# Another buffer for the second chunk's q, new durations for the norm's steps in a plan, and a new table of places (four interleaved attention layers, one core)

## The chip, the cores and the metric

The kernel runs on one core of a Trainium2 chip. Its engines are PE (TensorE, matrix products), DVE (VectorE), ACT (ScalarE), POOL (GpSimd) and SP (SyncE, which here only issues DMAs). The metric is the device time of one execution in microseconds; a kernel's time is the median of several runs.

## What is computed

Four layers in the order A, B, A, B are added to x, which has 2048 rows of 512 values in f32. Each layer is x + attention(layernorm(x)), with 32 heads of 16:

```python
def _A_ref(x, wqkv, wo):          # H = 32, Dh = 16, W = 8, dil = 2
    q, k, v = split(x @ wqkv)
    idx = pos[:, None] - off[None, :]      # off = 0, 2, ..., 14
    logits = einsum("bhsd,bhswd->bhsw", q, k[idx]) * scale
    attn = softmax(where(idx >= 0, logits, -1e9))
    return merge(einsum("bhsw,bhswd->bhsd", attn, v[idx])) @ wo
...
def _B_ref(x, wqkv, wo):          # W = 256
    scores = einsum("bhqd,bhkd->bhqk", q, k) * scale
    mask = (0 <= i - j) & (i - j < 256)
    p = softmax(where(mask, scores, -1e9))
    return merge(einsum("bhqk,bhkd->bhqd", p, v)) @ wo
...
x = x + _A_ref(_layernorm(x), A_wqkv, A_wo)
x = x + _B_ref(_layernorm(x), B_wqkv, B_wo)
x = x + _A_ref(_layernorm(x), A_wqkv, A_wo)
x = x + _B_ref(_layernorm(x), B_wqkv, B_wo)
```

In A each row looks at itself and seven rows before it, two apart; in B at the 256 rows that end with itself.

## The kernel before

Each layer is worked in eight chunks of 256 rows. A chunk of an A layer and a chunk of the B layer behind it run interleaved, so that the chunks of one layer's products fill the time of the other's elementwise work; a layer's next chunk starts when the rows that it needs are there. Products with weights are made of fp16 parts, high and low, so one product is three matmuls (L1014, L1015, L1016 with rows along the free axis; L1036, L1037, L1034 for the output projection).

The norm of a chunk: ACT makes the mean (L935) and the sum of squares (L938) of each of its two tiles of 128 rows, POOL makes from them the variance (L941), its root's inverse (L944) and the shift (L947). ACT normalizes (xn, L963 or L985) and casts to the high part (ht, L973); the remainder xn − ht (L969) runs on POOL or on DVE. In a layer A both parts go through DMAs that transpose them (xh, xl); for the first chunk and layer B, PE transposes (L989) and ACT and DVE cast (xh L994, xl L995).

A chunk of layer A then: PE makes q, k and v transposed, ACT copies q (L1130) and k, v with their halo (kv, L1132; halo copies L1122 and L1139 on POOL). For each of four groups of 128 channels (m = 0 to 3) and each of four stretches of 64 rows a product of q with the eight keys of its window (pr, L1151, 16 per chunk, 128x512, on DVE or POOL) is made, and PE reduces it over the 16 values of a head with a matrix of ones (L1159, four matmuls a group). The softmax over 8 is on DVE: maximum L1182, difference L1185, sum L1188, reciprocal L1191, scaling L1194, with the exponential on ACT (L1211); the result is cast (eh, L1215) and its remainder e − eh taken (L1202, DVE or POOL). PE spreads the weights over the heads' values (L1228), DVE weighs v (pw, L1241, eight per chunk, 128x1024), and the sums are taken on DVE (L1246) or in three steps on POOL (L1248, L1249, L1250). The finish: high part oh (L1058, ACT), remainder ol (L1060, DVE or POOL), projection, and the sum with x (y, L1068, DVE).

A chunk of layer B: k and q as high and low parts (eh L1272, el L1275), through DRAM into stacks (DMAs re L1285, stk L1296, both from SP's queue); a first pass of scores for the rows' maxima (L1338, L1341 on PE; mask and maximum L1359 and L1355 on DVE, or L1351 alone for a chunk without full tiles), the maxima transposed and split (mr L1374, mt L1381 to L1384) and added to the product by another row of the stack, the scores (L1431, L1433), the exponential (p, L1437, ACT), the mask (L1446, POOL), the product with v (L1463), and the division (os, L1480 to L1489).

What sets the order: every step is added to a plan with an engine, a duration in us, and what it reads and writes. Its place on its engine comes from a table, `ORDER[scope]`, by the step's number in its scope (the scopes are S, pA and pB for masks and weights, W for 110 groups of three idle matmuls, L1578, and A0 to A15, B0 to B15 for the chunks of the two A and the two B layers). A negative number puts the step on its second engine at place −1 − p. Each engine runs its steps strictly in the order of places. The durations serve `Plan.order()` alone: it plays the engines' queues against each other, gives buffers and PSUM banks as they come free in that play, and so sets the order in which the program is written and which bank a step gets.

Buffers come from pools by tag, in rotation. `po4` has one buffer for each of its tags: q, oa and ob. q of each A chunk takes the tag q, so a chunk's q may be written when the products of the chunk before have read theirs. `pp6` has one tag, p6, with three buffers of the same size: the staging of the output weights in the weight preparation, and later the probabilities p of layer B.

## Time and profile before

| | us |
|---|---|
| three runs: median (lowest to highest) | 1425.57 (1422.78 to 1426.98) |
| the profiled execution's own time | 1422.53 |
| its span in the profile | 1420.8 |
| PE busy in it | 1331.4 |
| DVE busy | 1125.9 |
| ACT busy | 818.9 |
| POOL busy | 697.2 |

The profile is one execution. Its span runs from the first to the last instruction that the profile shows, 1.7 us less than the execution's time. The mean granted clock of PE was 0.962 of the full one. "Busy" counts an engine's working instructions, not its waits and not the issuing of DMAs. A row of a view by line gives line, engine, operation, output and inputs with their shapes, how often, then the busy time of all, the mean of one in ns, the idle time of the engine just before them, and what ended that idle time.

The steps of the norm, whose durations in the plan the change sets anew, took in the trace: L935 628 ns with a read of its sum of 188 to 192 behind it, L938 720 with 188, L941 274, L944 741, L947 277, all means of 32 or 64.

### The profile page before, as it was taken

Reading aid. Unit: us, or ns where it says so; the run is one execution under the profiler, and the core shown is the slowest. Engines: PE = TensorE matmul, PEld = TensorE weight load, DVE = VectorE, ACT = ScalarE, POOL = GpSimd, SP = SyncE. Lnnn points to the kernel's source line nnn. Section 1 sums busy time; section 2 is a strip of 40 time slices with the busy share of each in tenths; the row PEclk is TensorE's granted clock in tenths of the full one; section 3 lists DMA queues with packets and bytes.
Section 4 is the critical chain, followed back from the end, with each engine's and each line's share of the span. In section 5 each row is a group of like instructions: output and inputs, shape, how many; then the busy total and the mean of one; then the engine's idle time right before and its main releaser. Section 6 shows DMA issues by size and latency. Waiting matters only on the chain.

```text
span 1420.8 us, 35345 instructions
## 1 busy us (share of the span) xinstructions
PE 1331.4 (94%) x13918; PEld 782.5 (55%) x13918; DVE 1125.9 (79%) x2087; ACT 818.9 (58%) x1297; POOL 697.2 (49%) x836
## 2 busy tenths in 40 slices
PE   9986989999899999999999898999989999998997
PEld 7642647456374654637465373745637465473644
DVE  7978796977969788796967759597796968879693
ACT  8732555565576557565675445656467555646564
POOL 4425182653747345373664627464272744738232
PEclk9996999999999999999999899998999999999999
DMA  8232333142342333324142252323324233233221
GB/s 267 67 101 58 108 66 104 47 103 85 97 132 49 105 84 88 101 73 137 45 116 78 59 136 67 108 77 88 99 74 135 53 92 87 72 107 85 95 73 58
DMA packets 135944, 130.46 MB, mean 92 GB/s; under 512 B 68448, under 2 KB 94560, under 8 KB 135776
## 3 DMA queue, kind: packets, MB, share of 16 engines
q1 hardware_dynamic: 135520, 127.93, 33.2%
q8 instruction: 109, 1.79, 0.5%
q14 instruction: 59, 0.48, 0.1%
q10 hardware_dynamic: 256, 0.26, 0.1%
HBM read 67.11 MB, written 43.48 MB: 78 GB/s over the span
## 4 chain that ended last, share of the span: by engine, by line
PE 60%; DVE 14%; POOL 7%; DMA 5%; issue 5%; ACT 5%; SPq 3%; DVEq 0%; POOLq 0%; ACTq 0%
PE banks L1014 9%; PE banks L1015 8%; PE banks L1016 8%; PE banks L1463 7%; PE banks L1036 5%; PE banks L1034 4%; PE banks L1431 4%; PE banks L1037 4%; PE banks L1159 4%; DVE m L1355 3%; PE banks L1338 3%; DVE pw L1241 3%; POOL pw L1248 3%; ACT p L1437 3%; PE banks L1341 2%
## 5 line engine op out<-in xcount | busy, mean ns | idle before, releaser
L1437 ACT ACTIVATE p<-banks,sclB 128x768 f32<-128x768 f32 x480 | 419.4, 901 | 246.5 <-PE banks L1433 172.8
L1446 POOL TENSOR_SCALAR_AFFINE_SELECT p<-p 128x1024 f32<-128x1024 f32 x240 | 262.8, 1103 | 315.7 <-ACT p L1437 304.1
L1355 DVE TENSOR_REDUCE m<-banks 128x2 f32<-128x512 f32 x448 | 296.0, 686 | 3.6
L1359 DVE COPY_PREDICATED banks<-maskt,banks 128x256 f32<-128x256 int16 x448 | 177.6, 423 | 72.3 <-PE banks L1341 57.6
L1463 PE MATMUL banks<-p,v 128*32 128x128 f32 (+1 forms) x3840 | 196.9, 334 | 5.3 <-POOL p L1446 4.7
L1151 DVE TENSOR_TENSOR pr<-kv,q 128x512 f32<-128x512 f32 x222 | 155.7, 752 | 42.9 <-PE banks L1159 27.8
L1463 PEld LDWEIGHTS banks<-p,v 128*32 128x32 f32 x3840 | 107.0, 110 | 96.7 <-issue 35.7
L1431 PE MATMUL banks<-stk,stk 64*128 64x256 f16 x960 | 133.3, 285 | 27.1 <-ACT p L1437 10.7
L1241 DVE TENSOR_TENSOR pw<-banks,kv 128x1024 f32<-128x1024 f32 x128 | 153.1, 1215 | 4.2 <-POOL o L1250 2.4
L1341 PE MATMUL banks<-stk,stk 48*128 48x128 f16 (+1 forms) x1024 | 127.0, 251 | 16.2 <-DVE m L1351 10.3
L1248 POOL TENSOR_TENSOR pw<-pw 128x512 f32<-128x512 f32 x100 | 127.2, 1272 | 10.5 <-DVE pw L1241 10.3
L1338 PE MATMUL banks<-stk,stk 48*128 48x256 f16 (+1 forms) x896 | 110.2, 253 | 18.0 <-DVE m L1355 9.4
L1431 PEld LDWEIGHTS <-stk 64*128 64x128 f16 x960 | 56.6, 95 | 121.4 <-issue 114.6
L1433 PE MATMUL banks<-stk,stk 64*128 64x128 f16 x960 | 108.2, 224 | 0.0
L1275 DVE SCALAR_TENSOR_TENSOR el<-banks,eh 128x512 f16<-128x512 f32 x64 | 43.2, 688 | 79.3 <-ACT eh L1272 49.9
L1338 PEld LDWEIGHTS <-stk 48*128 48x128 f16 x896 | 50.4, 95 | 94.3 <-issue 88.3
L1249 POOL TENSOR_TENSOR pw<-pw 128x256 f32<-128x256 f32 x100 | 72.7, 727 | 7.8
L1341 PEld LDWEIGHTS <-stk 48*128 48x128 f16 x1024 | 52.9, 96 | 35.2 <-issue 32.0
L1015 PE MATMUL banks<-xl,wA1h 128*128 128x256 f16 x256 | 69.8, 273 | 1.9 <-DMA xl<-xn 1.9
L1159 PE MATMUL banks<-pr,sel 128*32 128x512 f32 x512 | 70.6, 603 | 0.9 <-DVE y L1068 0.9
L1014 PE MATMUL banks<-xh,wA0h 128*128 128x256 f16 x256 | 70.1, 274 | 0.6 <-DMA xh<-ht 0.3
L1014 PE MATMUL banks<-xh,wA2h 128*128 128x256 f16 x256 | 70.4, 275 | 0.0
(201 smaller groups left out, 3110.8 us busy)
## 6 DMA issues: line engine op xcount, KB each, us to landing
stk<-re SPq DMA_DIRECT2D x256, 96.0 KB
re<-eh SPq DMA_DIRECT2D x128, 128.0 KB
xm<-y SPq DMA_DIRECT2D x32, 256.0 KB
re<-el SPq DMA_DIRECT2D x64, 128.0 KB
y<-xm SPq DMA_DIRECT2D x32, 256.0 KB
oc<-os SPq DMA_DIRECT2D x120, 64.0 KB
os<-scr SPq DMA_DIRECT2D x15, 512.0 KB
x<-in_A_x_dram SPq DMA_DIRECT2D x16, 256.0 KB
```

The lines of the kernel that those rows point to most:

```text
L1014: nc.tensor.matmul(ps[mp].t[:, i], wh, xh, start=k == 0, stop=False)
L1015: nc.tensor.matmul(ps[mp].t[:, i], wh, xl, start=False, stop=False)
L1241: nc.vector.tensor_mul(pw.t, pb.t.unsqueeze(1).broadcast_to([P, 2, W, 64]), v)
L1248: E.tensor_add(t[:, :, 0:4], t[:, :, 0:4], t[:, :, 4:8])
L1338: nc.tensor.matmul(ps.t[:, par, 0 : (2 - qb) * P], lhs, stk[hf, bef][r, col, qb * P :], start=True, stop=True)
L1341: nc.tensor.matmul(ps.t[:, par, (2 - qb) * P : 3 * P], lhs, stk[hf, now][r, col, : (1 + qb) * P], start=True, stop=True)
L1355: nc.vector.tensor_reduce(out=m.t[:, :, u, qb], in_=ps.t[:, :, 0 : 2 * P], op=ALU.max, axis=AX.X)
L1359: nc.vector.copy_predicated(t[:, :, 0:P], maskt[:, 0:P].bitcast(I16).unsqueeze(1).broadcast_to([P, 2, P]), t[:, :, 2 * P : 3 * P])
L1431: nc.tensor.matmul(o[:, two], k[:, jf * P : (jf + 1) * P], q, start=True, stop=True)
L1437: nc.scalar.activation(pt.t[:, :, 2 * i : 2 * i + 2].rearrange("p s m q -> p m s q"), ps.t[:, :, : 3 * P].rearrange("p m (s q) -> p m s q" ...
L1446: nc.gpsimd.affine_select(out=v, in_=v, pattern=[[0, 8], [-1 if b == 0 else 1, P]], compare_op=ALU.is_gt if b == 0 else ALU.is_ge, fill=0. ...
L1463: nc.tensor.matmul(o, v[:, jj, 17 * h : 17 * h + 32], rhs, start=z == 0 and (b == 0 or first), stop=z == 1 and b == 1, tile_position=(0, 3 ...
```

## The change

Three edits, none of which alters what an instruction computes.

1. In the first A layer, q of the second chunk takes a buffer of the tag p6 in `pp6` in place of the tag q in `po4`.
2. The plan's durations of the norm's five steps are set anew.
3. All scopes of the table ORDER have new numbers.

```diff
 ORDER = {
...
-    "A2": [12, 8, 20, 22, 14, 19, 14, 15, 16, 32, 34, -35, 61, 31, 38, 39, -47, 63, 30, 34, 42, 312, 314, 315, 319,
...
+    "A2": [10, 9, 16, 18, 15, 17, 13, 14, 16, 31, 32, -30, 29, 34, 28, 29, 18, 33, 31, 41, 43, 280, 292, 296, 311,
...
         for t in range(2):
-            plan.add("ACT", 0.72, lambda t=t: mean(t), r=[xs[t][1]], w=[vmean[t]])
-            plan.add("ACT", 0.9, lambda t=t: squares(t), r=[xs[t][1], vmean[t]], w=[vmv[t]])
-        plan.add("POOL", 0.25, spread_, r=vmv, w=[vr0[0]])
-        plan.add("POOL", 0.72, rstd, r=[vr0[0]], w=[vr0[1]])
-        plan.add("POOL", 0.3, shift, r=[vr0[1], *vmean], w=[vrs])
+            plan.add("ACT", 0.6, lambda t=t: mean(t), r=[xs[t][1]], w=[vmean[t]])
+            plan.add("ACT", 0.69, lambda t=t: squares(t), r=[xs[t][1], vmean[t]], w=[vmv[t]])
+        plan.add("POOL", 0.4, spread_, r=vmv, w=[vr0[0]])
+        plan.add("POOL", 0.6, rstd, r=[vr0[0]], w=[vr0[1]])
+        plan.add("POOL", 0.5, shift, r=[vr0[1], *vmean], w=[vrs])
...
         if l == 0 and c == 1:
 
-            q, o = buf("po4", [P, 4, C], F32, "q", f"q{l}_{c}"), buf("po4", [P, 4, C], F32, "ob", f"o{l}_{c}")
+            q, o = buf("pp6", [P, 4, C], F32, "p6", f"q{l}_{c}"), buf("po4", [P, 4, C], F32, "ob", f"o{l}_{c}")
```

The numbers of instructions on PE (21158) and SP (1236) stay the same, with the same matmuls and DMAs. Steps that can run on either engine change it: products L1151 on DVE 222 before and 230 now, on POOL 34 and 26; remainders L969 on DVE 14 and 22, on POOL 16 and 8; L1060 on DVE 19 and 17, on POOL 45 and 47; L1202 on DVE 9 and 7, on POOL 7 and 9.

Three places, in the rows in which each engine's instructions stand (line, operation, output <- inputs, shape; the numbers in a name are the chunk, the part and a running number, without the layer).

On PE in the run-in, before: the transposes of the first B chunk's normalized rows (L989), then six idle matmuls (two of their rows shown), then the first product with wB1.

```order
L1578 MATMUL banks<-idf 128x256
L989 MATMUL banks<-idf,xn_0_0_1111 128x128 x4
L989 MATMUL banks<-idf,xn_0_1_1114 128x128 x4
L1578 LDWEIGHTS idf
L1578 MATMUL banks<-idf 128x256
```

Now, the last product with wA1 for the third A chunk that stands ahead of them (21 stand there), the same transposes, the four reductions of the second group of the second chunk's products, and the first of three further matmuls with wA1 ahead of wB1:

```order
L1016 LDWEIGHTS wA1l
L1016 MATMUL banks<-xh_2_798,wA1l 128x256
L989 MATMUL banks<-idf,xn_0_1_1134 128x128 x4
L989 MATMUL banks<-idf,xn_0_0_1144 128x128 x4
L1159 MATMUL banks<-pr_1_1_0_1103,sel 32x512
L1159 MATMUL banks<-pr_1_1_1_1105,sel 32x512
L1159 MATMUL banks<-pr_1_1_2_1136,sel 32x512
L1159 MATMUL banks<-pr_1_1_3_1113,sel 32x512
L1014 LDWEIGHTS wA1h
L1014 MATMUL banks<-xh_2_798,wA1h 128x256
```

The wA1 products stood far behind wB1 before, the four reductions behind wB1 and the product with wB0; of 18 idle matmuls between the first group's reductions and wB1 six are left, ahead of the wA1 products.

On DVE in the run-in, before: the last products of the second A chunk, then its softmax (mx, e) and the first maximum of the first B chunk (m). The sum L1188 follows after four such maxima, L1191 after six and L1194 after eight.

```order
L1151 TENSOR_TENSOR pr_1_2_2_1298<-kv_1_1_793,q_1_809 128x512
L1151 TENSOR_TENSOR pr_1_2_1_1307<-kv_1_1_793,q_1_809 128x512
L1151 TENSOR_TENSOR pr_1_3_2_1318<-kv_1_1_793,q_1_809 128x512
L1151 TENSOR_TENSOR pr_1_3_1_1322<-kv_1_1_793,q_1_809 128x512
L1151 TENSOR_TENSOR pr_1_3_0_1328<-kv_1_1_793,q_1_809 128x512
L1151 TENSOR_TENSOR pr_1_3_3_1333<-kv_1_1_793,q_1_809 128x512
L1182 TENSOR_REDUCE mx_1_1345<-banks 128x64
L1185 TENSOR_TENSOR e_1_1349<-banks,mx_1_1345 128x512
L1351 ISA unread,m_0_0_1357<-banks,maskt 128x128
```

Now:

```order
L1275 SCALAR_TENSOR_TENSOR el_0_0_1325<-banks,eh_0_0_1311 128x2x256 x2
L1151 TENSOR_TENSOR pr_1_3_1_1334<-kv_1_1_638,q_1_846 128x512
L1151 TENSOR_TENSOR pr_1_3_3_1339<-kv_1_1_638,q_1_846 128x512
L1151 TENSOR_TENSOR pr_1_3_0_1342<-kv_1_1_638,q_1_846 128x512
L1151 TENSOR_TENSOR pr_1_3_2_1345<-kv_1_1_638,q_1_846 128x512
L1182 TENSOR_REDUCE mx_1_1355<-banks 128x64
L1185 TENSOR_TENSOR e_1_1362<-banks,mx_1_1355 128x512
L1188 TENSOR_REDUCE mx_1_1355<-e_1_1362 128x64
L1191 RECIPROCAL mx_1_1355<-mx_1_1355 128x64
L1194 TENSOR_TENSOR e_1_1362<-e_1_1362,mx_1_1355 128x512
L1351 ISA unread,m_0_0_1389<-banks,maskt 128x256
```

The last remainder el stands four products ahead of the softmax in place of six, and the five steps of the softmax stand together ahead of the first maximum; before the first L1241 stand ten maxima now, sixteen before.

On POOL in the second A chunk of the third layer, before: masks of the last B chunk of layer two (p), three products and a halo copy (ha).

```order
L1446 AFFINE_SELECT p_7_3_1_9772<-p_7_3_1_9772 128x1024
L1446 AFFINE_SELECT p_7_3_0_9824<-p_7_3_0_9824 128x1024
L1151 TENSOR_TENSOR pr_1_0_1_9896<-kv_1_1_8990,q_1_9864 128x512
L1151 TENSOR_TENSOR pr_1_0_3_9923<-kv_1_1_8990,q_1_9864 128x512
L1151 TENSOR_TENSOR pr_1_0_0_9942<-kv_1_1_8990,q_1_9864 128x512
L1139 COPY ha_1_1_9969<-kv_1_1_8990 128x56
L1446 AFFINE_SELECT p_7_4_0_9910<-p_7_4_0_9910 128x1024
```

Now:

```order
L1446 AFFINE_SELECT p_7_3_0_9813<-p_7_3_0_9813 128x1024
L1446 AFFINE_SELECT p_7_3_1_9768<-p_7_3_1_9768 128x1024
L1446 AFFINE_SELECT p_7_4_0_9917<-p_7_4_0_9917 128x1024
L1139 COPY ha_1_1_9971<-kv_1_1_8982 128x56
L1122 COPY kv_2_1_10130<-ha_1_1_9971 128x4x14
L1446 AFFINE_SELECT p_7_5_1_10082<-p_7_5_1_10082 128x1024
```

The three products stand on DVE.

834 rows, old and new, of the table ORDER are left out of this document.

## The prediction

> **What bounds the kernel now.** I read the page's busy shares first, then the chain that ended last, then windows of the steady part and the run-in.
>
> ```profile
> span 1420.8 us, 35345 instructions
> PE 1331.4 (94%) x13918; PEld 782.5 (55%) x13918; DVE 1125.9 (79%) x2087; ACT 818.9 (58%) x1297; POOL 697.2 (49%) x836
> PE 60%; DVE 14%; POOL 7%; DMA 5%; issue 5%; ACT 5%; SPq 3%; DVEq 0%; POOLq 0%; ACTq 0%
> ```
>
> PE is busy for 94% of the span and carries 60% of the chain. That leaves 1420.8 − 1331.4 = 89.4 us without a matmul, and any new order can only win from those and from time at a lowered clock. The windows show where they lie:
>
> ```profile
> 100.00:120.00 20.00, 10.64 (x54) 2.81 (x53) 16.72 (x55) 2.65 (x5) 6.09 (x8) 0.67 0.49 127
> 120.00:140.00 20.00, 15.06 (x93) 6.52 (x96) 16.11 (x50) 7.06 (x14) 13.93 (x16) 0.65 0.05 15
> 700.00:720.00 20.00, 17.99 (x173) 7.64 (x172) 19.86 (x34) 10.88 (x18) 19.29 (x24) 0.83 0.25 63
> 740.00:760.00 20.00, 20.00 (x243) 14.57 (x240) 8.61 (x16) 10.71 (x17) 7.70 (x9) 1.00 0.46 140
> 740.00:750.00 10.00, 10.00 (x117) 8.04 (x114) 1.29 (x2) 5.44 (x8) 2.51 (x4) 1.00 0.43 133
> 750.00:760.00 10.00, 10.00 (x129) 6.53 (x128) 7.32 (x14) 5.27 (x10) 5.20 (x5) 1.00 0.48 147
> ```
>
> (Columns: window, its length, busy us of PE, PEld, DVE, ACT, POOL, granted clock, DMA share, GB/s.) The steady part alternates. While an A chunk weighs its values (700 to 720) DVE is full, 19.86 of 20 us, and POOL nearly so, 19.29; PE loses 2.0 us and runs at 0.83. Elsewhere (740 to 760) PE is full and DVE has room, 8.61 of 20. The run-in (100 to 140) is the worst place: PE idles 9.4 + 4.9 us in two windows, at a clock of 0.67 and 0.65. So DVE work costs when it lies in the weighing stretch or in the run-in, and little elsewhere; POOL work likewise.
>
> The pace of the steady part is read from the start of each chunk's weighing; each row is one chunk's eight products of L1241, with the first and last start:
>
> ```profile
> L1241 DVE TENSOR_TENSOR pw<-banks,kv x8: 1184/1221/1225, 185.2 to 199.6; 128x1024 f32<-128x1024 f32 x8
> L1241 DVE TENSOR_TENSOR pw<-banks,kv x8: 1184/1216/1219, 440.3 to 455.6; 128x1024 f32<-128x1024 f32 x8
> L1241 DVE TENSOR_TENSOR pw<-banks,kv x8: 1185/1218/1225, 521.8 to 537.4; 128x1024 f32<-128x1024 f32 x8
> L1241 DVE TENSOR_TENSOR pw<-banks,kv x8: 1184/1208/1226, 607.2 to 623.7; 128x1024 f32<-128x1024 f32 x8
> L1241 DVE TENSOR_TENSOR pw<-banks,kv x8: 1182/1222/1228, 1029.0 to 1045.1; 128x1024 f32<-128x1024 f32 x8
> L1241 DVE TENSOR_TENSOR pw<-banks,kv x8: 1182/1215/1225, 1116.2 to 1133.3; 128x1024 f32<-128x1024 f32 x8
> ```
>
> From 185.2 to 607.2 are five periods of 84.4 us each on average; single ones are 521.8 − 440.3 = 81.5 and 1116.2 − 1029.0 = 87.2. So periods of the same work in different orders differ by about 3 us each way.
>
> **The change part by part.**
>
> *The buffer of q.* The old slot of the second chunk's q is free once the first chunk's products have read it. The view of the line shows what its copies wait for:
>
> ```profile
> L1130 ACT COPY q<-banks x32: 566/586/596, 25.4 to 1265.6; 128x512 f32<-128x512 f32 x32
>   PE banks L1016: 18.9, 22
> ```
>
> All idle time of ACT ahead of these copies ends with PE's matmuls, none with a reader of q. So no copy is late for want of a slot, and the edit alone is worth 0. The other way round, the new slot belongs to a rotation of three with the staging of weights and the probabilities; those first need it long after (the first probabilities come after the first mt at 114.59, quoted below). Bound: 0 to −0.8 us (less than two copies of 0.586). I take 0.
>
> *The durations of the norm.* They feed the planner only; no instruction carries them, so by themselves 0. What they do is in the table and in the merge of the engines' orders.
>
> *Work that changes engine.* Counted on the four engines' orders, 8 products of L1151 and 8 remainders of L969 go from POOL to DVE, and 2 remainders each of L1060 and L1202 go from DVE to POOL. The rows by line (busy us, mean ns):
>
> ```profile
> L1151 DVE TENSOR_TENSOR pr<-kv,q 128x512 f32<-128x512 f32 x222 | 155.7, 752 | 42.9 <-PE banks L1159 27.8 <-ACT kv L1132 8.7 <-ACT q L1130 6.2
> L1151 POOL TENSOR_TENSOR pr<-kv,q 128x512 f32<-128x512 f32 x34 | 44.6, 1325 | 51.3 <-PE banks L1159 29.4 <-ACT q L1130 16.8 <-ACT kv L1132 5.1
> L969 POOL TENSOR_TENSOR xn<-xn,ht 128x512 f16<-128x512 f32 x16 | 18.9, 1182 | 36.8 <-ACT ht L973 27.4 <-PE banks L1433 5.3 <-PE banks L1463 4.1
> L969 DVE TENSOR_TENSOR xn<-xn,ht 128x512 f16<-128x512 f32 x14 | 10.1, 721 | 2.2 <-ACT ht L973 2.2
> L1060 DVE TENSOR_TENSOR ol<-oc,oh 128x512 f16<-128x512 f32 x18 | 13.1, 738 | 5.2 <-ACT oh L1058 5.1
> ```
>
> DVE gains 8 × 0.752 + 8 × 0.721 − 4 × 0.738 = 8.8 us (L1202 taken at L1060's duration, the same shape); POOL loses 8 × 1.325 + 8 × 1.182 = 20.1 us and takes up four remainders again. Does it lie where DVE is full? The remainders do not: each of those that DVE now has in the steady part stands behind the eighth L1241 of a chunk. The products come ahead of the first. In the third layer's second chunk, which had three products on POOL and now has none there, that stage looked like this:
>
> ```profile
> 750.12 3.93 POOL L1151 TENSOR_TENSOR pr<-kv,q 128x512 f32<-128x512 f32 x3 [3.24 <-ACT kv L1132]
> 750.43 0.76 DVE L1359 COPY_PREDICATED banks<-maskt,banks 128x256 f32<-128x256 int16 x2 [2.19 <-ACT kv L1132]
> 751.83 1.17 DVE L1151 TENSOR_TENSOR pr<-kv,q 128x512 f32<-128x512 f32 x1
> 755.49 1.29 DVE L1151 TENSOR_TENSOR pr<-kv,q 128x512 f32<-128x512 f32 x2 [0.61 <-PE banks L1159]
> 759.72 2.50 DVE L1151 TENSOR_TENSOR pr<-kv,q 128x512 f32<-128x512 f32 x4 [1.36 <-PE banks L1159]
> ```
>
> (Start, length, engine, line; in brackets the idle time before and what ended it.) DVE idles 2.19 + 0.61 + 1.36 = 4.2 us there while PE is full (10.00 of 10 in both windows above), and three products more take 3 × 0.75 = 2.3 us. So the cover is DVE's own waiting for PE, and most of the 8.8 us costs nothing. Without that cover it would be all 8.8 us. A gain is possible too, by POOL's relief: one product of DVE beside POOL's three took 1.17 us where two others took 1.29 together, so each product that leaves POOL may spare DVE some 0.5 us; 16 such moves, 8 us, which would cancel the cost. Bounds −1 to +8.8; I take +1, near the covered end.
>
> The Trainium skill's page "SBUF — State Buffer", section "🔬 SBUF: two separate sides", says that DVE and GpSimd share one port pair as an exclusive lock for the whole instruction, where a DVE operation with two SBUF inputs meets a GpSimd operation that reads SBUF. The 1.17 us product agrees with it; by the rule in full the moves would be worth about 0 instead of +1, and the sum one us lower.
>
> *The run-in.* Here the new order differs in a way that can be followed step by step. The rows of the time before:
>
> ```profile
> 75.72 1.51 PE L1159 MATMUL banks<-pr,sel 128*32 128x512 f32 x7
> 77.15 1.48 PE L1578 MATMUL banks<-idf 128*128 128x256 f16 x12
> 80.30 1.36 PE L989 MATMUL banks<-idf,xn 128*128 128x128 f32 x8 [1.66 <-ACT xn L985]
> 83.06 0.27 PE L1015 MATMUL banks<-xl,wB1h 128*128 128x256 f16 x1 [0.42 <-DVE xl L995]
> 94.64 1.29 DVE L1275 SCALAR_TENSOR_TENSOR el<-banks,eh 128x512 f16<-128x512 f32 x2 [2.54 <-DMA re<-eh]
> 95.85 2.27 DVE L1151 TENSOR_TENSOR pr<-kv,q 128x512 f32<-128x512 f32 x2
> 98.94 2.50 DVE L1151 TENSOR_TENSOR pr<-kv,q 128x512 f32<-128x512 f32 x4 [0.83 <-PE banks L1159]
> 102.58 0.69 DVE L1182 TENSOR_REDUCE mx<-banks 128x64 f32<-128x512 f32 x1 [1.14 <-PE banks L1159]
> 105.45 1.01 DVE L1188 TENSOR_REDUCE mx<-e 128x64 f32<-128x512 f32 x1
> 108.62 0.69 DVE L1194 TENSOR_TENSOR e<-e,mx 128x512 f32<-128x512 f32 x1
> 113.49 1.18 DVE L1241 TENSOR_TENSOR pw<-banks,kv 128x1024 f32<-128x1024 f32 x1
> 114.59 0.18 DVE L1384 SCALAR_TENSOR_TENSOR mt<-mr,mt 128x32 f16<-128x32 f32 x1
> ```
>
> First, PE. It waited 1.66 us for xn and stood on fillers before. Now 24 matmuls of the third chunk's k and the four reductions of the products' second group stand ahead of wB1, with 6 fillers in place of 18. At 1.48 / 12 = 0.12 us a matmul and 1.51 / 7 = 0.22 us a reduction: 21 of the matmuls and the 6 fillers take 3.3 us from about 77.15, so L989 starts near 80.5 (80.30 before), and the four reductions and three matmuls add 0.9 + 0.4 behind it, against 0.7 for six fillers. wB1's second matmul waited until 83.06 anyway, so wB1 is 0.2 to 0.7 us late: that delays el, and SP's re and stk transfers queued behind it, by as much. What it buys is 24 × 0.12 = 2.9 us of matmuls done where PE would idle.
>
> Second, DVE. Six products stood between the last el and the maximum L1182; now four do. Two products and one wait less: 0.83 + 2.27 = 3.1 us, so L1182 moves from 102.58 to about 99.5, plus the 0.2 to 0.7 of wB1. The five softmax steps stood among the mask reductions L1351, 6.0 us from L1182 to L1194; now they stand together, at 0.69 + 0.69 + 1.01 + about 0.55 = 2.9 us. L1194 starts near 102.9 instead of 108.62. From there to the first L1241 were 4.9 us, which gives 107.8, but ten L1351 steps now stand ahead of it on DVE, at about 0.55 us each, so 109: 4.5 us early. Third, the price: the first mt of layer B, which PE's scores wait for, has three of L1241 ahead of it instead of one. It begins 3 us earlier and has 2 × 1.2 us more, plus wB1's delay: −0.7 to +1.4 against 114.59. The run-in ends when both are through. If the weighing sets the end it is 4.5 us shorter, if mt does 1.4 longer. In the window 120 to 140 POOL is at 13.93 of 20 with the totals behind L1241, and PE has 4.9 us idle, so I hold the weighing for the likelier; what follows it on PE is shared, so I take −2.5, with −4.5 and +1.4 as ends.
>
> *The rest of the table.* Nearly every step has a new place, but the same work per period. The two periods above show what an order does: −3 to +3 each. Over some 14 periods without a common sign this gives a scatter of 3/2 × √14 = 6 us as an estimate, its mean 0. The tail has the same order but for three fillers fewer: 0.4 us at most.
>
> **The sum**, against the profiled execution's own 1422.53 us (span 1420.8 and 1.7 around it): 0 + 0 + 1 − 2.5 + 0 = −1.5, so 1421.0. That execution was 3.0 under the median of 1425.57, and 0.25 under the fastest of the three runs, so a median of the changed kernel should stand 0 to 3 above the sum; I put it at a third: 1422 us.
>
> **The rivals.**
>
> (1) *DVE's cover fails* (slower). DVE pays where it is full: the moved products delay the softmax and thereby the weighing, and the mt of the run-in comes 1.4 late. It decides once the products of a chunk end later than PE's reductions of them, that is when the 4.2 us of waiting in that stage are less than the added 2.3. For it: 19.86 of 20 in the weighing. Against it: the waits above. 1422.5 + 8.8 + 1.4 = 1432.7, with the median's 1 on top 1434.
>
> (2) *A larger gain.* The remainder on DVE ends 1.18 − 0.72 = 0.46 us earlier ahead of the transposes, and the new order evens the periods. If the two or three long periods (87.2) come down to 84.4, that is 2 × 2.8 = 5.6, with the whole 4.5 of the run-in: 1422.5 − 10.1 + 1, about 1414. For it: the spread is there. Against it: each period has its own halo and tail work, and the windows do not show that the long ones lose to order.
>
> (3) *It does nothing*: q's slot was never waited for, and the run-in's gain is taken up by the next wait of PE. About 1425, the median before.
>
> **How the numbers follow.** Forecast 0.40, its own range 1417 to 1427; rival (1) 0.25; (2) 0.20; (3) 0.15. About 0.3%, 4.3 us, is what a measurement of this kernel tells from none: faster lies below 1421.3, slower above 1429.8. The forecast gives 0.16 to faster and 0.24 to same; (2) gives all its 0.20 to faster; (3) 0.14 to same and 0.01 to slower; (1) its 0.25 to slower. Faster 0.36, same 0.38, slower 0.26. The range reaches to both outer cases, 1412 to 1435.
>
> **What would show it.** Right: the first L1241 of the second chunk in the run-in at about 109 (113.49 before), L1182 near 100, and wB1 no later than 83.8; q's copies still wait for PE alone; DVE's busy time about 9 us up and POOL's 15 down or more; the mean of the periods from the first L1241 to the next at 84 to 85. Wrong: the weighing stretch of single chunks longer by more than a us, DVE waits of the products for PE gone and new PE waits on DVE's softmax, or the first mt after 116.

## The result and the profile after

The changed kernel takes 1429.93 us (median of 20 executions, 1424.80 to 1432.72), the kernel before 1425.01 beside it (1421.06 to 1428.54): a ratio of 1.0032, 95% interval 1.0019 to 1.0044, so 4.6 us slower. (The ratio is estimated from all executions; it is not the quotient of the two medians, which differ by 4.9 us.) The forecast was 1422, faster. The profiled execution took 1430.58 us, 1428.9 of them in the span, at the same mean granted clock as before, 0.962.

The head of the page, busy shares and chain:

```profile
span 1428.9 us, 35335 instructions
PE 1337.7 (94%) x13918; PEld 786.1 (55%) x13918; DVE 1138.7 (80%) x2102; ACT 816.6 (57%) x1294; POOL 683.5 (48%) x824
PE 48%; DVE 10%; POOL 5%; DMA 5%; issue 4%; SPq 4%; ACT 4%; ACTq 0%; POOLq 0%; DVEq 0%
```

PE's time without a matmul hardly grew (1428.9 − 1337.7 = 91.2 us, 89.4 before); the other 6.3 us of the span are time in which the record has PE busy, with the same 13918 matmuls. The shares of this chain add up to 80% of the span, those of before to 99%, so they are not compared. DVE has 12.8 us more (9 forecast), POOL 13.7 less (15 forecast).

The two windows of the run-in that were shown of before (window, length, busy us of PE, PEld, DVE, ACT, POOL, clock, DMA share, GB/s):

```profile
100.00:120.00 20.00, 13.74 (x69) 3.85 (x67) 15.47 (x46) 2.74 (x5) 3.60 (x4) 0.86 0.54 145
120.00:140.00 20.00, 12.62 (x68) 5.00 (x65) 17.45 (x47) 5.57 (x9) 16.18 (x19) 0.63 0.05 15
```

PE is busier in the first, 13.74 against 10.64, and emptier in the second, 12.62 against 15.06. The gain of the new order is there and is given back.

The products of L1241, from which the pace is read (number, times of one, first and last start): the first two chunks of A together, the third and the last, of the kernel before,

```profile
L1241 DVE TENSOR_TENSOR pw<-banks,kv x16: 1181/1215/1225, 54.0 to 126.9; 128x1024 f32<-128x1024 f32 x16
L1241 DVE TENSOR_TENSOR pw<-banks,kv x8: 1181/1218/1227, 1283.2 to 1298.4; 128x1024 f32<-128x1024 f32 x8
```

and of the changed one:

```profile
L1241 DVE TENSOR_TENSOR pw<-banks,kv x16: 1182/1214/1225, 58.6 to 131.0; 128x1024 f32<-128x1024 f32 x16
L1241 DVE TENSOR_TENSOR pw<-banks,kv x8: 1203/1208/1214, 191.1 to 205.5; 128x1024 f32<-128x1024 f32 x8
L1241 DVE TENSOR_TENSOR pw<-banks,kv x8: 1181/1208/1217, 1294.6 to 1309.5; 128x1024 f32<-128x1024 f32 x8
```

These starts cut an execution into four stages: the *start* up to the first L1241, the *run-in* up to the third chunk's first L1241 (185.2 before, 191.1 now), the *steady* part up to the last chunk's, and the *tail* to the span's end. All profiled executions of this study, in us (each figure rounded by itself), with the median, the median of the kernel before beside it, and their ratio:

| kernel | start | run-in | steady | tail | span | median / before | ratio [95%] |
|---|---|---|---|---|---|---|---|
| before | 54.0 | 131.1 | 1098.0 | 137.6 | 1420.8 | | |
| changed | 58.6 | 132.5 | 1103.4 | 134.3 | 1428.9 | 1429.93 / 1425.01 | 1.0032 [1.0019, 1.0044] |
| changed again (after2) | 57.9 | 131.5 | 1102.6 | 136.2 | 1428.3 | 1434.01 / 1425.12 | 1.0068 [1.0050, 1.0086] |
| changed again (after3) | 58.5 | 132.9 | 1099.5 | 134.4 | 1425.3 | 1431.21 / 1424.98 | 1.0041 [1.0025, 1.0056] |
| aq4 | 58.3 | 131.8 | 1101.8 | 136.8 | 1428.7 | 1430.47 / 1425.12 | 1.0037 [1.0020, 1.0054] |
| q6 | 54.8 | 133.5 | 1099.0 | 137.3 | 1424.5 | 1426.07 / 1425.12 | 1.0010 [0.9996, 1.0024] |
| dur | 55.9 | 132.8 | 1102.8 | 134.9 | 1426.4 | 1430.15 / 1425.12 | 1.0043 [1.0027, 1.0059] |
| dur_bb | 54.6 | 133.0 | 1100.6 | 136.1 | 1424.4 | 1424.02 / 1425.39 | 0.9994 [0.9980, 1.0007] |
| h24_p | 57.7 | 133.7 | 1099.3 | 136.3 | 1426.9 | 1429.37 / 1424.98 | 1.0031 [1.0018, 1.0044] |
| h60 | 55.4 | 131.8 | 1100.7 | 138.1 | 1426.0 | 1426.51 / 1422.43 | 1.0033 [1.0018, 1.0048] |
| h160 | 56.7 | 135.4 | 1099.1 | 136.8 | 1427.9 | 1427.79 / 1422.43 | 1.0036 [1.0021, 1.0051] |
| r60 | 59.0 | 131.9 | 1106.1 | 136.1 | 1433.1 | 1434.57 / 1422.43 | 1.0090 [1.0072, 1.0108] |
| r60_bb | 60.3 | 132.6 | 1100.4 | 135.9 | 1429.2 | 1429.72 / 1425.28 | 1.0030 [1.0010, 1.0051] |
| r140 | 58.3 | 137.7 | 1109.0 | 134.7 | 1439.7 | 1441.39 / 1422.43 | 1.0138 [1.0117, 1.0159] |
| r140_bb | 58.4 | 134.4 | 1104.7 | 136.6 | 1434.1 | 1436.24 / 1425.28 | 1.0088 [1.0063, 1.0113] |
| st_rest_p | 59.3 | 132.5 | 1102.4 | 134.1 | 1428.4 | 1432.17 / 1425.39 | 1.0058 [1.0040, 1.0077] |
| st_prod_p | 61.4 | 132.0 | 1101.2 | 136.9 | 1431.5 | 1432.81 / 1425.39 | 1.0057 [1.0043, 1.0072] |
| st_both_p | 62.5 | 131.4 | 1100.1 | 137.0 | 1431.0 | 1432.92 / 1425.39 | 1.0059 [1.0037, 1.0080] |
| st_act_p | 57.7 | 132.3 | 1102.5 | 137.0 | 1429.5 | 1430.96 / 1424.98 | 1.0033 [1.0018, 1.0047] |
| st_act2_p | 57.9 | 133.5 | 1101.5 | 135.0 | 1427.9 | 1430.33 / 1424.98 | 1.0036 [1.0023, 1.0050] |

A stage of one profile scatters, and the changed kernel's own ratio, taken at three times, stands at 1.0032, 1.0068 and 1.0041; smaller differences between rows of different times say little. So means of several executions are compared. The old order with the old PSUM banks (before, q6, dur_bb; a PSUM bank is one of the eight that the plan hands out for PE's results) against the new table (changed three times, aq4): start 54.5 and 58.3, run-in 132.5 and 132.2, steady 1099.2 and 1101.8, tail 137.0 and 135.4. The differences, +3.8, −0.3, +2.6 and −1.6, add up to 4.6 us between the mean spans. Three more executions have the old order in the start, but other banks for 35 steps of PE there (dur, h60, h160): their start takes 55.4 to 56.7, 56.0 in the mean, where the three with the old banks lie at 54.0 to 54.8.

The start, in which the largest of the differences lies, in rows of the time (start, length, engine, line; in brackets the idle time before and what ended it). The kernel before:

```profile
26.66 1.88 DVE L1151 TENSOR_TENSOR pr<-kv,q 128x512 f32<-128x512 f32 x3
...
28.53 0.68 DVE L1151 TENSOR_TENSOR pr<-kv,q 128x512 f32<-128x512 f32 x1
29.13 0.27 DVE L854 TENSOR_REDUCE a1A<-banks 2x1 f32<-2x128 f32 x1
34.25 1.28 DVE L909 SCALAR_TENSOR_TENSOR wA2l<-stk,pscA,wA2h 128x1024 f16<-128x1024 f32 x1 [1.29 <-ACT wA2h L911]
40.96 1.22 SPq L820 DMA_DIRECT2D stageB<-in_B_wo_dram  x2
46.86 1.06 ACT L830 ACTIVATE wB3l<-stageB 128x1024 bf16<-128x1024 f32 x1 [1.00 <-DMA stageB<-in_B_wo_dram]
```

The changed one:

```profile
24.47 2.19 POOL L969 TENSOR_TENSOR xn<-xn,ht 128x512 f16<-128x512 f32 x1 [2.45 <-ACT ht L973]
27.76 2.15 POOL L969 TENSOR_TENSOR xn<-xn,ht 128x512 f16<-128x512 f32 x1
25.57 2.17 DVE L832 CUSTOM_DVE_ANT_0 wA3l<-stageA 128x1024 bf16<-128x1024 f32 x1
28.89 4.33 DVE L1151 TENSOR_TENSOR pr<-kv,q 128x512 f32<-128x512 f32 x4
33.14 0.27 DVE L854 TENSOR_REDUCE a1A<-banks 2x1 f32<-2x128 f32 x1
38.12 1.28 DVE L909 SCALAR_TENSOR_TENSOR wA2l<-stk,pscA,wA2h 128x1024 f16<-128x1024 f32 x1
44.34 1.21 SPq L820 DMA_DIRECT2D stageB<-in_B_wo_dram  x2
50.90 1.06 ACT L830 ACTIVATE wB3l<-stageB 128x1024 bf16<-128x1024 f32 x1 [2.19 <-DMA stageB<-in_B_wo_dram]
```

The weights' scale (L854) comes 4.0 us late, behind four products as before, which take 4.33 us in place of 1.88 + 0.68. The low part of wA2 is 3.9 late, SP's staging of layer B's wo 3.4 (its buffer holds the staging of layer A until DVE has made a part of wA3 from it), and ACT's L830, which waits for that staging, 4.0. The exponential of the first chunk's softmax stands two steps behind L830 on ACT, and the first L1241 comes 4.6 us late. Three remainders are made on POOL in this stage, one before; beside them DVE's work stretches.

### The profile page after: what moved, and what is told of

Its sections match the earlier page's. It is cut to its first block, busy times and chain, and to the rows that moved or that the text cites. A ratio compares the mean times of both kernels' runs of the same rounds, so it can differ in the third digit from the quotient of the medians.

```text
span 1428.9 us, 35335 instructions
## 1 busy us (share of the span) xinstructions
PE 1337.7 (94%) x13918; PEld 786.1 (55%) x13918; DVE 1138.7 (80%) x2102; ACT 816.6 (57%) x1294; POOL 683.5 (48%) x824
## 4 chain that ended last, share of the span: by engine, by line
PE 48%; DVE 10%; POOL 5%; DMA 5%; issue 4%; SPq 4%; ACT 4%; ACTq 0%; POOLq 0%; DVEq 0%
PE banks L1014 6%; PE banks L1463 6%; PE banks L1016 6%; PE banks L1015 6%; PE banks L1036 4%; PE banks L1034 4%; PE banks L1037 3%; PE banks L1431 3%; PE banks L1159 3%; PE banks L1338 3%; ACT p L1437 2%; DVE m L1355 2%; POOL pw L1248 2%; PE banks L1341 2%; DVE banks L1359 2%
## 5 line engine op out<-in xcount | busy, mean ns | idle before, releaser
L1359 DVE COPY_PREDICATED banks<-maskt,banks 128x256 f32<-128x256 int16 x448 | 178.0, 422 | 58.7 <-PE banks L1341 54.8
L1151 DVE TENSOR_TENSOR pr<-kv,q 128x512 f32<-128x512 f32 x230 | 156.8, 731 | 41.8 <-PE banks L1159 24.8
L1431 PE MATMUL banks<-stk,stk 64*128 64x256 f16 x960 | 136.3, 286 | 23.6 <-DVE m L1355 6.8
L1241 DVE TENSOR_TENSOR pw<-banks,kv 128x1024 f32<-128x1024 f32 x128 | 153.1, 1212 | 3.5 <-PE banks L1228 1.8
L1341 PE MATMUL banks<-stk,stk 48*128 48x128 f16 (+1 forms) x1024 | 129.9, 253 | 12.4 <-DVE m L1351 6.5
L1338 PE MATMUL banks<-stk,stk 48*128 48x128 f16 (+1 forms) x896 | 113.1, 254 | 25.4 <-DVE m L1355 11.0
L1014 PE MATMUL banks<-xh,wA1h 128*128 128x256 f16 x256 | 70.1, 274 | 2.0 <-DVE el L1275 0.8
L1015 PE MATMUL banks<-xl,wA1h 128*128 128x256 f16 x256 | 69.8, 273 | 1.1 <-DMA xl<-xn 1.1
```

The lines of the kernel that those rows point to most:

```text
L1014: nc.tensor.matmul(ps[mp].t[:, i], wh, xh, start=k == 0, stop=False)
L1015: nc.tensor.matmul(ps[mp].t[:, i], wh, xl, start=False, stop=False)
L1151: E.tensor_mul(pr.t, window(kv[1].t, m, 64 * tq, 64)[:, 0], qb)
L1338: nc.tensor.matmul(ps.t[:, par, 0 : (2 - qb) * P], lhs, stk[hf, bef][r, col, qb * P :], start=True, stop=True)
L1341: nc.tensor.matmul(ps.t[:, par, (2 - qb) * P : 3 * P], lhs, stk[hf, now][r, col, : (1 + qb) * P], start=True, stop=True)
L1359: nc.vector.copy_predicated(t[:, :, 0:P], maskt[:, 0:P].bitcast(I16).unsqueeze(1).broadcast_to([P, 2, P]), t[:, :, 2 * P : 3 * P])
```

## The experiments

**The table in pieces.** Is the loss one of the start or of the rest? Steps that the plan starts before a cut stand in one table's order on each engine, the rest behind them in the other's; code as in the changed kernel. h60 and h160: the old table for the first 53 and 160 us; r60 and r140: the new one for the first 53 and 135 us.

```diff
-ORDER = (the new table)
+ORDER = (per engine: the steps before the cut in the order of table 1, then the rest in the order of table 2)
```

> The changed kernel with the table of before for the steps of the first 53 us (weight preparation and the first A chunk up to its first L1241), on each engine, and the changed table behind them; q in p6 and the new durations stay. Theory 'start': the loss lies in those first steps, since in the profiles the first L1241 stands at 58.6 us after and 54.0 before. Then this kernel takes 1425 us or less (about 4.6 below the changed kernel's 1429.9), its first L1241 at 54 to 55. Rival 'steady': the products and remainders moved to DVE cost in the steady part (1103.5 us from the third chunk's first L1241 to the last chunk's, 1098.0 before). Then it stays at 1429 to 1430.

> The changed kernel with the table of before for all steps of the run-in and of the third chunk's beginning (the first 160 us of the plan), the changed table behind them. Theory 'start': 1425, as before, since only the start costs. Rival 'steady': 1429 to 1430, since the whole steady part is the changed one.

> The reverse of h60: the changed table for the first 53 us, the table of before behind them. Theory 'start': 1429.5, 4.6 above before, with the first L1241 at 58 to 59. Rival 'steady': 1425, the time before.

> The changed table for the first 135 us (the whole run-in to the second A chunk's last output rows), the table of before behind them. Theory 'start': 1429 to 1430 (the 4.6 us of the start, less what the run-in behind it wins, at most 2.7 by the profiles: first L1241 of the second chunk 1.9 late instead of 4.6). Rival 'steady': 1425 or less.

All four are slower than the kernel before: +0.33%, +0.36%, +0.90% and +1.38%. The start follows the order that it has (55.4 and 56.7 with the old one, 59.0 and 58.3 with the new). But what was saved in the start by h60 does not show in its total, and r60 and r140 lose 7 and 10 us in the steady part (against 1099.2), where they hold the old table. A piece of a table does not keep its time when what stands ahead of it is another: something besides the order on the engines changed with it.

**The edits one by one.** q6 is the kernel before with edit 1 alone, dur with edit 2 alone; aq4 is the changed kernel without edit 1; after2 is the changed kernel again.

```diff
q6, on the kernel before:
-            q, o = buf("po4", [P, 4, C], F32, "q", f"q{l}_{c}"), ...
+            q, o = buf("pp6", [P, 4, C], F32, "p6", f"q{l}_{c}"), ...
dur, on the kernel before (and L941, L944, L947 likewise to 0.4, 0.6, 0.5):
-            plan.add("ACT", 0.72, lambda t=t: mean(t), ...
-            plan.add("ACT", 0.9, lambda t=t: squares(t), ...
+            plan.add("ACT", 0.6, lambda t=t: mean(t), ...
+            plan.add("ACT", 0.69, lambda t=t: squares(t), ...
aq4, on the changed kernel:
-            q, o = buf("pp6", [P, 4, C], F32, "p6", f"q{l}_{c}"), ...
+            q, o = buf("po4", [P, 4, C], F32, "q", f"q{l}_{c}"), ...
```

> The changed kernel itself, as the reference for what runs beside it. All theories: 0.2 to 0.45% above before.

> The kernel before with edit 1 alone: the second chunk's q in a buffer of p6, all else as before. Theory 'slot' (the buffer itself matters, since p6 also serves the staging of layer B's output weights and the probabilities): 2 to 5 us above before. Rival 'table' (only the new places cost): 0, within 0.1% of before, because q was never waited for in its old slot.

> The kernel before with edit 2 alone: the norm's new durations in the plan, with the old table. On each engine every step stays at its place; what can move is which bank of PSUM and which buffer a step gets and the order between engines. Theory 'table': 0, within 0.1% of before. Rival 'play' (the engines' orders cost nothing by themselves, but the play of the plan hands out banks by its own times, and a table fits one play alone): 3 to 10 us above before, as r60 and r140 were 8 to 11 us longer than before from the third chunk on with the old places.

> The changed kernel without edit 1: q of the second chunk in its old slot of po4, new durations and new table. Theory 'slot': 2 to 5 us below the changed kernel. Rival 'table': the same as the changed kernel within 0.1%, or above it by up to 1.5 us if the new order has q's copy ahead of the first chunk's last product.

q's buffer is worth nothing in the kernel before: q6 1.0010 [0.9996, 1.0024]. In the changed kernel it is not settled: aq4 (1.0037, twelve executions) is 3.5 us faster by the medians than after2 beside it (1.0068, six), as the theory 'slot' expected, but the changed kernel's other two measurements (1.0032 and 1.0041) lie where aq4 does. And dur, in which every step keeps its place on its engine, is 6.1 us slower (1.0043 × 1425.12), 3.8 to 8.4 by the interval. The durations change the play in `Plan.order()`, and that play hands out the PSUM banks: of the 3560 steps on PE that hold a bank, 422 get another one (160 of the 1604 bank buffers). What the trace shows of it, in the waits of PE between the weighings of the first layer's fourth and fifth chunk, about 354 to 448 (line and what it waited for: us in all, times, longest); before:

```profile
PE banks L1338 <- DVE m L1355: 1.6, 3, 0.6
PE banks L1431 <- DVE pw L1241: 1.6, 2, 0.9
PE banks L1338 <- ACT p L1437: 0.6, 1, 0.6
```

and dur:

```profile
PE banks L1338 <- ACT p L1437: 1.6, 2, 1.0
PE banks L1431 <- DVE pw L1241: 1.2, 2, 0.7
PE banks L1338 <- DVE m L1355: 0.9, 2, 0.6
...
PE banks L1431 <- ACT p L1437: 0.6, 1, 0.6
```

PE's first pass of scores and its scores now wait for exponentials that have not yet emptied their bank, 2.2 us against 0.6. The sum of the waits moves less than that, yet this period takes 89.3 us (357.8 to 447.1) against 86.3 (354.0 to 440.3).

**The same with the banks held.** dur_bb is dur, in which each step takes the bank that it has in the kernel before.

```diff
+BANK = {scope: {(step, buffer): bank}}     (of the kernel before, where they differ)
...
-    for t in plan.order():
+    seq = plan.order()
+    (each bank buffer of each step: at = BANK[scope][step, buffer], where it is listed)
+    for t in seq:
```

> The kernel dur (before with the norm's new durations in the plan) with the banks of PSUM that the kernel before hands out, all else as dur. Between dur and before 422 of 3560 steps of PE that hold banks have other ones, and the steps of different engines are written in another order. Theory 'banks': the 0.43% of dur are gone, the time is within 0.1% of before. Rival 'written order': it stays 4 to 6 us above before.

0.9994 [0.9980, 1.0007]: the loss is gone, and the same period is 86.1 us again (356.5 to 442.6). Of the waits for the exponentials one is left there:

```profile
PE banks L1338 <- ACT p L1437: 0.5, 1, 0.5
```

dur_bb keeps dur's order of writing the steps of different engines, so that order costs nothing that shows, and dur's 6 us are those of the banks. (dur and dur_bb were measured at different times, each beside the kernel before; the 0.49% between them is more than the 0.36% by which the changed kernel's own ratio spread, and the two pairs that follow go the same way.) The cut tables were then run with the banks of the kernel before wherever both have the old order (from 60.6 us in r60_bb, from 155 in r140_bb; 137 bank buffers in each, which are 361 and 354 of the steps on PE).

> r60 (changed table for the first 53 us, table of before behind them) with the banks of before from 60.6 us on; 137 of 1604 bank buffers change against r60. Theory 'banks and start': 3 us above before (the start's 58.4 against 55.4), 9 under r60; from the third chunk's first L1241 to the last chunk's 1098 us instead of 1105.8. Rival 'order' (the old table does not fit the changed start, whatever the banks): 8 us or more above before.

> r140 (changed table for the first 135 us, table of before behind them) with the banks of before from 155 us on; 137 of 1604 bank buffers change. Theory 'banks and start': the steady part takes 1098 us instead of 1109.1, so 11 under r140's 19 above before: 8 above, of which 3 are the start and the rest the seam (82 us from the second to the third chunk's first L1241 in r140 against 72 to 76 elsewhere). Rival 'order': 15 us or more above before.

r60 falls from +12.8 us to +4.3 (1.0030 [1.0010, 1.0051]), with its steady part at 1100.4, near that of before: 8.5 us were 137 bank buffers, and 4.3 us, 1.4 to 7.3 by the interval, are what the new order of the first 53 us costs with its seam and with the banks that go with it there, which were not held. r140 falls from +19.6 to +12.5 us and keeps a steady part of 1104.7; what its seam costs there was not found.

**Which steps of the start cost.** Each takes the changed kernel, with its banks held (in st_act_p and st_act2_p but for one bank buffer, in h24_p but for five), and puts a few steps back. st_rest_p: three remainders L969 from POOL to DVE. st_prod_p: five products behind the scale's steps L854 to L873 on DVE, the first reduction behind them on PE. st_both_p: both. st_act_p: ACT's L938 (two) and L935 of the third chunk behind the cast wA1h (L911). st_act2_p: that and the second half of the first chunk's xh and xl behind the squares. h24_p: the old table for the first 24 us.

```diff
-ORDER = (the new table)
+ORDER = (the new table with these few steps elsewhere; in h24_p those of the first 24 us)
```

> The changed kernel with three remainders L969 of the start (second chunk's two, one of the third's) on DVE, as before, in place of POOL; banks as in the changed kernel. Theory 'contention': beside these three on POOL (2.15, 2.19, 1.46 us each) DVE's L832 took 2.17 instead of 1.22 and four products 4.33 us instead of 2.5; moved to DVE they cost 3 x 0.69 = 2.1 and give back 0.9 + 1.8 and part of the waits behind them: first L1241 at 56.5 to 57.5 (58.4 in the mean of five executions with the changed start), the time 1 to 2 us under the changed kernel's 1.004 of before. Rival 'order' (the four products ahead of the scale of the third and fourth weight set the delay): no change, 58 or later.

> The changed kernel with five products L1151 of the first chunk behind the scale of the weights of k2 and the output (L854 to L873) on DVE, and their first reduction behind it on PE; banks as in the changed kernel. Theory 'order': L854 stood at 33.1 behind 4.3 us of products; now it comes near 29, the splits L909 of the output weights 2 to 4 us earlier, and with them SP's second load of layer B's output weights, which ACT waited 2.2 us for; first L1241 at 55 to 56.5, the time 2 to 3 us under the changed kernel. Rival 'contention': the products are only late and as slow, first L1241 at 58 or later.

> Both edits of st_rest_p and st_prod_p. If both causes are real: first L1241 at 54 to 55.5, as with the start of before, the time 3 us under the changed kernel: 1.001 to 1.003 of before. If neither: 58.4 and 1.004.

> The changed kernel again, as the reference on this chip: 1.003 to 1.007 of before, first L1241 at 58 to 59.

> The changed kernel with three of the third chunk's norm steps on ACT (two L938 and one L935) behind the splits wA1h (L911), as before; banks as in the changed kernel but for one. Theory 'ACT': seven steps of 0.78 us each from start to start stand ahead of wA1h, where the plan counts 0.6 and 0.69; without three of them wA1h starts 2.3 us earlier (18.5 instead of 20.9), wA1l on DVE and all behind it likewise, and the first L1241 comes at 56 to 57, the time 2 to 3 us under the changed kernel beside it. Rival 'later': DVE and SP are late for other reasons, first L1241 at 58 or more, the time as the changed kernel's within 1 us.

> st_act_p, and the second half of the first chunk's xh and xl behind the weights' squares on ACT and DVE, as before, which lets the first weight's scale (L873) go ahead of it. If that order counts too: 1.2 us more than st_act_p, first L1241 at 55 to 56, the time 3 to 4 us under the changed kernel. If not: as st_act_p.

> The changed kernel with the old table for the steps of the first 24 us of the plan on all engines, banks as in the changed kernel but for five. If the delay is made in these 24 us: first L1241 at 55 to 56 and the time 3 us under the changed kernel beside it. If it is made behind them (the loads of layer B's weights on SP, the products): 58 and the same time.

None brings the start back. st_rest_p takes the cause of the stretch away, and its DVE shows that (four products, then the scale):

```profile
28.07 1.22 DVE L832 CUSTOM_DVE_ANT_0 wA3l<-stageA 128x1024 bf16<-128x1024 f32 x1
30.43 2.49 DVE L1151 TENSOR_TENSOR pr<-kv,q 128x512 f32<-128x512 f32 x4
32.84 0.27 DVE L854 TENSOR_REDUCE a1A<-banks 2x1 f32<-2x128 f32 x1
```

2.49 us for four products instead of 4.33, 1.22 for L832 instead of 2.17; yet the scale gains only 0.3 us, since the remainders take their place on DVE and the first of them waits 1.28 us for ACT. The start ends at 59.3. In st_prod_p the scale comes early, but its user does not:

```profile
29.33 0.28 DVE L854 TENSOR_REDUCE a1A<-banks 2x1 f32<-2x128 f32 x1 [0.36 <-PE banks L848]
38.74 1.28 DVE L909 SCALAR_TENSOR_TENSOR wA2l<-stk,pscA,wA2h 128x1024 f16<-128x1024 f32 x1
42.12 2.50 DVE L1151 TENSOR_TENSOR pr<-kv,q 128x512 f32<-128x512 f32 x4 [1.98 <-ACT q L1130]
```

wA2's low part is no earlier than 38.12, and ACT's copy of q now comes late for DVE: 61.4. The two on ACT and h24_p (57.7, 57.9, 57.7) stand at the lower edge of the changed kernel's 57.9 to 58.6, and their ratios are within 0.1% of its ratio beside them (after3). So neither the contention nor the late scale by itself makes the start late; read from the traces, several waits of about the same length lie beside each other. One of them none of these runs takes away: ACT's cast of wA2's high part (L911), which wA2's low part needs, begins at 35.52 in the changed kernel and at 33.08 in the kernel before, and ahead of it ACT waits 1.22 and 2.45 us for the transposing DMAs of earlier remainders (xl from xn). Between 24 and 40 us all fourteen executions with the new order there have 2.0 to 3.9 us of this wait; of the six with the old order only h160 has any, 1.3. Whether it decides was not tested, and which set of steps would have to move back stays open. Nothing in the study is faster than the kernel before; dur_bb and q6 cannot be told from it.

## Why the prediction was wrong, step by step

**The start was not read.** The prediction opened the order at 75 us. The new table differs from the first instruction on, and the first 53 us, in which the kernel before has DVE busy for 30.8 of the 34 us from 20 to 54, cost 3.8 us by the profiles and 4.3 by r60_bb. Both figures hold the order and the banks that go with it: the old order with other banks for 35 steps is by itself 1.5 us later (56.0 against 54.5, three executions each), and how the 3.8 divide was not measured. That term is missing from the sum, and it is its largest. The count that stood in its place hid it: "8 remainders from POOL to DVE" is a net number, and in the start two remainders more than before stand on POOL, beside a DVE that is busy for 9.9 of the 10 us from 24 to 34.

**The run-in: −2.5 forecast, −0.3 measured.** Its steps in the profiled execution of the changed kernel:

```profile
88.58 0.27 PE L1014 MATMUL banks<-xh,wB1h 128*128 128x256 f16 x1
97.29 3.52 DVE L909 SCALAR_TENSOR_TENSOR wB3l<-stageB,pscB,wB3h 128x1024 f16<-128x1024 f32 x1
97.42 2.30 POOL L1151 TENSOR_TENSOR pr<-kv,q 128x512 f32<-128x512 f32 x2
101.46 1.29 DVE L1275 SCALAR_TENSOR_TENSOR el<-banks,eh 128x512 f16<-128x512 f32 x2 [0.65 <-DMA re<-el]
106.31 0.69 DVE L1182 TENSOR_REDUCE mx<-banks 128x64 f32<-128x512 f32 x1 [1.16 <-PE banks L1159]
108.51 1.03 DVE L1188 TENSOR_REDUCE mx<-e 128x64 f32<-128x512 f32 x1 [0.79 <-ACT e L1211]
110.17 0.69 DVE L1194 TENSOR_TENSOR e<-e,mx 128x512 f32<-128x512 f32 x1
115.43 1.22 DVE L1241 TENSOR_TENSOR pw<-banks,kv 128x1024 f32<-128x1024 f32 x1
121.78 0.18 DVE L1384 SCALAR_TENSOR_TENSOR mt<-mr,mt 128x32 f16<-128x32 f32 x1
```

The steps are counted from the first L1241 of the first chunk (54.05 before, 58.61 now), since all of the run-in begins late. One execution against one misleads here: the second chunk's weighing stands 59.4 us after that mark in the kernel before, but 61.6 and 61.2 in q6 and dur_bb, which have its order and its banks. So the figures are means of before, q6 and dur_bb, and of the changed kernel's three executions and aq4.

- wB1 was to be 0.2 to 0.7 us late. Its first matmul stands at 28.4 and 29.3: 0.9 late. The last el is 0.8 late.
- L1182 was to gain 3.1 less wB1's delay, so 2.4 to 2.9: 49.2 and 47.0, so 2.2. The mechanism is right, and the size nearly so.
- From L1182 to L1194 it takes 3.9 us, 6.9 before and 2.9 forecast: the wait for ACT's exponential, 0.79 in the rows above, which four maxima had filled before, was left out.
- The second chunk's first L1241: 60.8 and 56.1, 4.7 earlier, where 4.5 was forecast.
- The first mt: 61.9 and 62.4, 0.5 late, inside the range of −0.7 to +1.4. That range does not follow from its terms, though: 3 us earlier, 2 × 1.2 later and wB1's 0.2 to 0.7 give −0.4 to +0.1. At 121.78 the mt is past the 116 that was named as the sign of a wrong forecast, but q6 and dur_bb, which lose no time, have it at 117.5 and 117.0: the sign could not tell.
- The third chunk's first L1241, with which the run-in ends: 132.5 and 132.2. It stands 71.8 behind the second chunk's weighing before and 76.1 now, but 70.7 and 69.8 behind the first mt.

So the step that fell is the choice ahead of the sum, that the weighing sets the end of the run-in and not mt. The weighing came as early as forecast, the mt hardly moved, and the end of the run-in stayed with the mt. All twenty profiled executions divide in this way: with the new run-in the second chunk's weighing comes 55.5 to 56.8 us after the first chunk's and the third's 75.7 to 82.0 after that; with the old one it is 59.1 to 61.6 and 71.6 to 74.9. What lies between shows in after2, where the second chunk's weighing begins at 113.47 as it did before at 113.49, but the first mt at 119.8 and not at 114.59. The window from 130 to 150, before and then in after2:

```profile
130.00:150.00 20.00, 18.70 (x152) 11.07 (x151) 14.38 (x54) 11.25 (x22) 6.68 (x9) 0.90 0.10 29
```

```profile
130.00:150.00 20.00, 17.43 (x113) 7.71 (x113) 14.79 (x68) 7.19 (x16) 8.39 (x12) 0.76 0.01 2
```

PE gets 113 matmuls done where it did 152, at a clock of 0.76 in place of 0.90, and ACT, whose exponentials stand behind the scores, 7.19 us of work in place of 11.25. From the same beginning the third chunk's weighing starts at 189.5 against 185.2: 4.3 us given back. That mt is what makes PE late there is read from this order of events; no run moved mt alone.

**"The durations: by themselves 0"** was wrong as a step. No instruction carries them, but they decide the banks: dur +6.1 us, dur_bb −0.9 [−2.8, +1.0]. In the changed kernel another table is played with them, and 2781 of the 3560 steps have another bank, so how much of its steady +2.6 us is banks and how much is order was not separated: holding the old banks under the new table was not tried.

**The buffer of q, 0:** right for the kernel before, by q6; in the changed kernel aq4 leaves it open between 0 and 3.5 us. The view of the line shows no copy of the changed kernel that waits for a reader of q:

```profile
L1130 ACT COPY q<-banks x32: 552/585/609, 25.7 to 1277.4; 128x512 f32<-128x512 f32 x32
...
  PE banks L1016: 17.8, 16
```

**DVE's moved work, +1:** the size holds in the place that it was read from, and rival (1) is not what happened. The groups by line after (busy us, mean ns, idle time before and what ended it):

```profile
L1151 DVE TENSOR_TENSOR pr<-kv,q 128x512 f32<-128x512 f32 x230 | 156.8, 731 | 41.8 <-PE banks L1159 24.8 <-ACT kv L1132 13.5 <-ACT q L1130 3.2
L1151 POOL TENSOR_TENSOR pr<-kv,q 128x512 f32<-128x512 f32 x26 | 35.0, 1354 | 48.5 <-PE banks L1159 41.4 <-ACT q L1130 4.6 <-ACT kv L1132 2.6
L969 DVE TENSOR_TENSOR xn<-xn,ht 128x512 f16<-128x512 f32 x22 | 15.4, 710 | 4.9 <-ACT ht L973 4.3 <-issue 0.7
```

Eight products more cost DVE 1.1 us in place of 6.0, as the mean fell from 752 to 731 ns: the relief by POOL that the prediction had as its lower bound. DVE's products still wait 24.8 us for PE (27.8 before). In the third layer's second chunk, which has all sixteen products on DVE now,

```profile
761.97 1.29 DVE L1151 TENSOR_TENSOR pr<-kv,q 128x512 f32<-128x512 f32 x2 [3.90 <-ACT kv L1132]
778.32 0.69 DVE L1182 TENSOR_REDUCE mx<-banks 128x64 f32<-128x512 f32 x1
```

the way from DVE's first product to the maximum is 16.4 us, and was 15.7 (751.83 to 767.56): 0.6 for three products more, not 2.3. From the chunk's first product on either engine, POOL's at 750.12, it had been 17.4. The row of the kernel before:

```profile
767.56 0.69 DVE L1182 TENSOR_REDUCE mx<-banks 128x64 f32<-128x512 f32 x1
```

**The rest of the table, 0 ± 6, its tail 0.4 at most:** +2.6 in the steady part, −1.6 in the tail. The mean period is (1294.6 − 191.1) / 13 = 84.9 us, 84.5 before, inside the 84 to 85 that were to show the forecast right. It was too coarse a test: 0.4 us in 13 periods is 5 us.

Of the rivals none has it. (1) came nearest in time (1434) by another mechanism; (3), at 1425, was right that the run-in's gain is taken up behind it, and saw neither the start nor the banks; of (2) nothing came.

## What to carry to other kernels

A new table is compared from its first instruction on, and by stage and direction: a net count of moved steps hides that a few went the other way in the fullest stretch. A planner's durations are part of the kernel where its play hands out buffers or banks; before a new order is judged, hold the hand-out fixed, or the two are measured as one. Where a step is put earlier, ask what the end of the stage waits for: here one layer's weighing came 4.7 us earlier, the other layer's mt did not, and the stage ended as late as before. And read such steps from several executions: one execution of each kernel alone gives 2.6 us for the weighing, and the mt 2.6 us late.

## What the runs showed of the hardware

With the same order on every engine, other PSUM banks for 422 of 3560 steps cost 0.4% (dur against dur_bb), and for 361 steps 0.6% (r60 against r60_bb); the visible part is PE waiting for a bank that its reader has not left.

The two halves of wB3's low part took DVE 2.47 us before. In the changed kernel the second took 3.52 by itself, in the rows of the run-in above, where POOL, already at work on a copy (L1122) when DVE's step begins, makes two products in 2.30 us beside it. One of the two halves takes 3.52 to 3.56 in all thirteen executions with the new run-in, and none more than 1.28 in the seven others. Such a step takes 1.28 elsewhere (wA2's in the start), and 1.28 + 2.30 = 3.58: one after the other. The Trainium skill's page "SBUF — State Buffer", section "🔬 SBUF: two separate sides", has DVE and GpSimd take one shared port pair in turn, as a lock; this row agrees with it, and the 1.22 and 2.17 us of L832 without and with POOL's remainders beside it agree in kind.
